# Attention ordered by query tile over all heads, v projection within its own batch, and batch 1 transposed on TensorE

## The chip, the cores and the metric

The kernel runs on one core of one Trainium2 chip. The metric is the device time of that core in microseconds (us); lower is better. Engines are named as in the profile: PE (TensorE, matrix products), PEld (its weight loads, which overlap PE: 12.83 us of them in a batch of 29.84 us in which PE is busy throughout), DVE (VectorE), ACT (ScalarE), POOL (GpSimd), SP (SyncE, which only issues DMAs here). The span of an execution is the time from its first instruction to its last; in these runs the time is the span plus 1.7 to 1.9 us (283.9 and 285.62, 262.4 and 264.19).

## The reference, cut to what matters

There are 8 batches, 16 query heads on 4 kv heads, 384 positions, head dimension 64, model width 1024. Attention comes first, then a gated feed-forward whose gate mixes the positions.

```python
k = np.repeat(k, group, axis=1); v = np.repeat(v, group, axis=1)      # group = 4
scores = np.matmul(q, k.transpose(0, 1, 3, 2)) / np.sqrt(D)
attn = softmax(scores)
x = (attn @ v).transpose(0, 2, 1, 3).reshape(B, S, H * D)
h = np.maximum(x @ w_in, 0.0);  u, v = h[..., :512], h[..., 512:]
v_n = (v - mean(v)) / np.sqrt(var(v) + 1e-06)
v_s = np.einsum('ts,bsd->btd', w_spatial, v_n) + b_spatial[None, :, None]
out = (u * v_s) @ w_out
```

## The kernel before

Each batch is a row of nine visits. A visit starts with two units of scores (two 64-row products each) and their exps on ScalarE, and then gets other PE work to fill the time of those exps. That work is: the value products and sums of exps (`values`, giving `sums` and `X`), the v half of the projection (`pv`), the spatial product with w_spatial (`psp`), the u half (`pu`) and the output product (`po`). Four PSUM buffers (`ps`) are shared by all of them, and VectorE or ScalarE frees them.

Before the change a value product covers one head over all 384 positions and a call of `values` four heads, so a batch has four calls with 384 columns:

```python
def values(b, gp, quad, part=None):
    ...
    def tiles(dst, weights):
        for t in range(NST):
            for i in range(4):
                half, j = i // 2, quad * 2 + i % 2
                nc.tensor.matmul(dst[32 * i : 32 * (i + 1), 0:S], weights(t, half),
                                 a[:, t, half, j * S : (j + 1) * S], ...)
    ...
VALUES_AT = {0: (-1, 1, 1), 3: (0, 0, 0), 5: (0, 0, 1), 8: (0, 1, 0)}

def feed_forward(b, vi):          # the feed-forward of batch b-1 and b-2 in the visits of b
    ...
    if vi == 1: do_v(b - 1, 0, 1)
    if vi == 2: do_v(b - 1, 2)
    ...
    if vi == 2: do_o(b - 2, 0)
    if vi == 3: do_o(b - 2, 1)
    if vi == 4: do_o(b - 2, 2, 3, 4)
    if vi == 5: do_o(b - 2, 5)
    if vi == 6: do_sp(b - 1)
    if vi == 7: do_u(b - 1, 0, 1)
    if vi == 8: do_u(b - 1, 2)
```

Batch 0 is ordered by hand on PE, POOL, SP and also DVE. From batch 1 on, DVE is left to the scheduler of the framework, which may place a DVE instruction anywhere that its dependences and its priorities allow:

```python
def load_w_in(c0, c1):            # 16 DMAs of 64 KB a half, on GpSimd's queue, casting to fp16
    for gp in range(2):
        for half in range(2):
            for quad in range(2):
                ...
                for jq in range(2):
                    nc.gpsimd.dma_start(...)

def cast_ws():                    # waits for the load of w_spatial
    for tt in range(NST):
        nc.vector.tensor_copy(ws16[:, tt, :, :], ...)

def first_visit(vi):              # batch 0
    ...
    if vi == 4:
        cast_k(1, nc.vector)
        cast_q(1, 0, nc.vector)
        load_ws()
        load_bias()
    if vi in (6, 7): transpose_k(1, vi - 6)
    if vi in (7, 8): transpose_q(1, 0, vi - 7)
    if vi == 8:
        values(0, 1, 0, 0)
        dma_transpose_q(1, 1)     # the second half of batch 1's q, by a DMA
        cast_ws()                 # the last DVE work ordered by hand

with tc.manual_schedule(engines={PE, POOL, SP, DVE}):
    ...                           # batch 0
with tc.manual_schedule(engines={PE, POOL, SP}):
    ...                           # batches 1 to 7
```

The softmax here doesn't subtract the row's maximum and nothing guards it: scores larger than these inputs give would overflow.

Of the kernel before, what the change touches and what calls it, by code (L numbers as in the profile page):

```python
# [19 lines left out]
def kernel(  # L20
# [19 lines left out]
    nc = tc.nc  # L40
# [50 lines left out]

    def load_k(b):
        k32 = ld.tile([P, HKV, NST * D], FP32, name=f"k32_{b}", tag="k32")
        nc.sync.dma_start(k32, k[b].rearrange("g (p t) d -> p g (t d)", t=NST))
        loaded["k32", b] = k32

    def load_v(b):
        v32 = ld.tile([P, HKV, NST * D], FP32, name=f"v32_{b}", tag="v32")
        nc.sync.dma_start(v32, v[b].rearrange("g (p t) d -> p g (t d)", t=NST))
        loaded["v32", b] = v32  # L100

    def load_q(b, gp, pieces=1):
        q32 = ld.tile([P, 2 * G, NST * D], FP32, name=f"q32_{b}_{gp}", tag=f"q32_{gp}")
        n = 2 * G // pieces
        for i in range(pieces):
            h0 = gp * 2 * G + i * n
            nc.sync.dma_start(
                q32[:, i * n : (i + 1) * n, :],
                q[b, h0 : h0 + n].rearrange("h (p t) d -> p h (t d)", t=NST),
            )  # L110
        loaded["q32", b, gp] = q32

    def cast_k(b, engine):
        k16 = qk16.tile([P, NGP, NST, 2, D], FP16, name=f"k16_{b}", tag="k16")
        k32 = loaded["k32", b].rearrange("p (gp h) (t d) -> p gp t h d", gp=NGP, t=NST)
        for gp in range(NGP):
            engine.tensor_copy(k16[:, gp], k32[:, gp])  # L117
        loaded["k16", b] = k16

    def cast_v(b, engine):  # L120
        v16 = qk16.tile([P, HKV, NST, D], FP16, name=f"v16_{b}", tag="v16", bufs=3)
        engine.tensor_copy(v16.rearrange("p g t d -> p g (t d)"), loaded["v32", b])
        loaded["v16", b] = v16

    def cast_q(b, gp, engine):
        q16 = qk16.tile([P, G, NST, 2, D], FP16, name=f"q16_{b}_{gp}", tag=f"q16_{gp}")
        q32 = loaded["q32", b, gp]
        for half in range(2):
            engine.tensor_copy(
                q16[:, :, :, half, :],  # L130
                q32[:, half * G : (half + 1) * G, :].rearrange("p j (t d) -> p j t d", t=NST),
            )
        loaded["q16", b, gp] = q16

    def load_first():


        k32 = ld.tile([P, HKV, NST * D], FP32, name="k32_0", tag="k32")
        q32 = ld.tile([P, 2 * G, NST * D], FP32, name="q32_0_0", tag="q32_0")

        def piece(queue, i):
            queue.dma_start(
                q32[:, 2 * i : 2 * i + 2, :],
                q[0, 2 * i : 2 * i + 2].rearrange("h (p t) d -> p h (t d)", t=NST),
            )

        def kpiece(gp):
            nc.sync.dma_start(
                k32[:, 2 * gp : 2 * gp + 2, :],
                k[0, 2 * gp : 2 * gp + 2].rearrange("g (p t) d -> p g (t d)", t=NST),  # L150
            )

        kpiece(0)
        piece(nc.scalar, 0)
        piece(nc.sync, 2)
        piece(nc.sync, 1)
        piece(nc.sync, 3)
        load_v(0)
        load_q(0, 1, pieces=2)
        kpiece(1)  # L160

        k16 = qk16.tile([P, NGP, NST, 2, D], FP16, name="k16_0", tag="k16")
        q16 = qk16.tile([P, G, NST, 2, D], FP16, name="q16_0_0", tag="q16_0")
        k32v = k32.rearrange("p (gp h) (t d) -> p gp t h d", gp=NGP, t=NST)
        q32v = q32.rearrange("p (h j) (t d) -> p j t h d", h=2, t=NST)
        nc.vector.tensor_copy(k16[:, 0], k32v[:, 0])  # L166
        nc.scalar.activation(q16[:, 0:2, :, 0, :], q32v[:, 0:2, :, 0, :], AF.Copy)
        nc.vector.tensor_copy(q16[:, 0:2, :, 1, :], q32v[:, 0:2, :, 1, :])
        nc.vector.tensor_copy(q16[:, 2:4, :, 0, :], q32v[:, 2:4, :, 0, :])
        nc.gpsimd.tensor_copy(q16[:, 2:4, :, 1, :], q32v[:, 2:4, :, 1, :])  # L170
        cast_v(0, nc.gpsimd)
        cast_q(0, 1, nc.gpsimd)
        nc.gpsimd.tensor_copy(k16[:, 1], k32v[:, 1])
        loaded["k16", 0] = k16
        loaded["q16", 0, 0] = q16

    def load_batch(b):
        load_k(b)
        load_q(b, 0)
        cast_k(b, nc.gpsimd)  # L180
        cast_q(b, 0, nc.gpsimd)
        load_v(b)
        load_q(b, 1)
        cast_v(b, nc.gpsimd)
        cast_q(b, 1, nc.gpsimd)

# [9 lines left out]
    def load_consts():  # L196
        make_identity(nc, ident16)
        nc.vector.memset(ones32, 1.0)
        nc.vector.memset(eps_t, eps_ln)

    def load_bias():
        nc.sync.dma_start(bias_b, moe_b_spatial.partition_broadcast(P))

    def load_w_in(c0, c1):

        for gp in range(2):
            for half in range(2):
                for quad in range(2):
                    r0 = (gp * 2 * G + half * G + 2 * quad) * D
                    rows = moe_w_in[r0 : r0 + 2 * D, c0:c1].rearrange(  # L210
                        "(jq jj r) n -> jq r jj n", jq=2, jj=2
                    )
                    kc = gp * 4 + quad * 2
                    for jq in range(2):
                        i = half * 2 + jq
                        nc.gpsimd.dma_start(  # L216
                            w_in16[32 * i : 32 * (i + 1), kc : kc + 2, c0:c1], rows[jq]
                        )
# [8 lines left out]
    def load_ws():  # L227
        ws32 = stage.tile([P, NST, S], FP32, name="ws32", tag="ws32", bufs=1)
        nc.sync.dma_start(ws32, moe_w_spatial.rearrange("(p tt) s -> p tt s", tt=NST))
        loaded["ws32"] = ws32  # L230

# [17 lines left out]
    kT, qT, aT, xT = {}, {}, {}, {}  # L249

    def dma_transpose_k(b):
        kT[b] = tr_sb.tile([P, NGP, NST, P], FP16, name=f"kT_{b}", tag="kT")
        nc.sync.dma_start_transpose(
            kT[b].rearrange("p g t q -> p (g t) q"),
            loaded["k16", b].rearrange("p g t h d -> p (g t h d)"),
        )

    def dma_transpose_q(b, gp):
        qT[b, gp] = tr_sb.tile([P, G, NST, P], FP16, name=f"qT_{b}_{gp}", tag=f"qT_{gp}", bufs=2)
        nc.sync.dma_start_transpose(  # L260
            qT[b, gp].rearrange("p j t q -> p (j t) q"),
            loaded["q16", b, gp].rearrange("p j t h d -> p (j t h d)"),
        )

    def transpose_k(b, gp):
        k16 = loaded[("k16", b)]
# [3 lines left out]
        if gp == 0:  # L270
            kT[b] = tr_sb.tile([P, NGP, NST, P], FP16, name=f"kT_{b}", tag="kT")
        nc.vector.tensor_copy(kT[b][:, gp], pk)

    def transpose_q(b, gp, jp):
        q16 = loaded[("q16", b, gp)]
        if jp == 0:
            qT[b, gp] = tr_sb.tile([P, G, NST, P], FP16, name=f"qT_{b}_{gp}", tag=f"qT_{gp}", bufs=2)
        pq = ps.tile([P, 2, NST, P], FP16, name=f"pq_{b}_{gp}_{jp}", tag="ps")
        for jj in range(2):
            for t in range(NST):  # L280
                nc.tensor.transpose(
                    pq[:, jj, t, :],
                    q16[:, 2 * jp + jj, t, :, :].rearrange("p h d -> p (h d)"),
                    ident16,
                )
        nc.vector.tensor_copy(qT[b, gp][:, 2 * jp : 2 * jp + 2, :, :], pq)

    def scores(b, units):
        scs = []
        for u in units:  # L290
            gp, c, t = u // 9, (u % 9) // 3, u % 3
            sc = ps_sc.tile([P, 2, 512], FP32, name=f"sc_{b}_{u}", tag="sc")
            rhs = qT[b, gp].rearrange("p j t q -> p (j t q)")
            for half in range(2):
                lo, hi = half * D, (half + 1) * D
                nc.tensor.matmul(  # L296
                    sc[:, half, :],
                    kT[b][lo:hi, gp, t, :],
                    rhs[lo:hi, c * 512 : (c + 1) * 512],
                    start=True,  # L300
                    stop=True,
                )
            scs.append((gp, c, t, sc))
        for gp, c, t, sc in scs:
            if (b, gp) not in aT:
                aT[b, gp] = att_a.tile(
                    [P, NST, 2, G * S], FP16, name=f"aT_{b}_{gp}", tag="aT"
                )
            nc.scalar.activation(  # L309
                aT[b, gp][:, t, :, c * 512 : (c + 1) * 512], sc, AF.Exp, scale=scale  # L310
            )

    def values(b, gp, quad, part=None):


        a = aT[b, gp]
# [147 lines left out]
    def do_v(b, *sts):  # L464
        for st in sts:
            mk_v(b, st)()
# [145 lines left out]
```

## Time and profile before

| Reading | Value | How to read it |
|---|---|---|
| Time | 267.97 us (266.47 to 268.8, three runs) | 268.38 with the run beside the changed kernel |
| Span of the profiled execution | 270.2 us, mean granted clock 0.983 | a longer execution than any fast run on record: those of this kernel have spans of 264.1 to 270.1 us and clocks of 0.986 to 1.0 |
| Steady batch | 29.84 us, all of it PE busy, clock 1.00 | PE bound; any PE time saved here counts six times. The mean of the six is 29.94; one of them takes 30.57, with a wait of 0.7 us for a DMA transpose |
| First scores of batch 1 | at 28.64 us | all of the start and batch 0 lie before it |

From the page of the kernel before: busy us of each engine, share of the span and instructions; then two rows of slices. The digits are tenths of busy time, one for each fortieth of the span (6.75 us); PEclk is the granted clock in the same way.

```profile
PE 250.0 (93%) x2233; PEld 109.6 (41%) x2233; DVE 139.0 (51%) x273; ACT 185.0 (68%) x250; POOL 54.4 (20%) x90
...
PE   1887993989999999999999899999999999999993
...
PEclk9998898899999999999999999999999999999998
```

PE is at 8 tenths or more from the eighth slice on, up to the last. What is left to win lies in the first seven slices, in the last one, or in doing less PE work.

One steady batch of the kernel before, from the table of stretches. The columns are the stretch, its length, then busy time and count of PE, PEld, DVE, ACT and POOL, the granted clock, the DMA share and GB/s.

```profile
59.82:89.66 29.84, 29.84 (x274) 12.83 (x276) 15.71 (x31) 23.29 (x32) 4.94 (x7) 1.00 0.63 174
```

PE has no idle time in it, and no other engine comes near 29.84 us.

The two waits of PE above 1 us, from the list of waits of the kernel before (total, times, longest, in us):

```profile
PE pk_0_158 L269 <- DVE k_0_129 L166: 4.5, 1, 4.5
PE sc_9_698 L296 <- DMA qT_1_464<-q_1_1_238: 4.1, 1, 4.1
```

The first is the start of the kernel. The second is batch 1 waiting for its second q half from the DMA transpose: the wait that the change sets out to remove.

VectorE around the end of batch 0 in the kernel before, from its timeline (start, busy us, then what it is; in brackets the idle time before it and what ended that):

```profile
18.94 1.02 DVE L129 CAST q_1_0_324<-q_1_0_192 128x768 f16<-128x768 f32 x2
...
29.74 1.90 DVE L236 CAST ws_466<-ws_327 128x384 f16<-128x384 f32 x3 [0.30 <-DMA ws_327<-in_moe_w_spatial_dram]
```

The casts for batch 1 are done by 20 us. The cast of w_spatial (`ws`) comes only when everything that batch 1 needs at its start is out of the way, and its data has landed by then; VectorE waited 0.3 us for it.

### The profile page before, as it was taken

Reading aid. Unit: us, or ns where it says so; the run is one execution under the profiler, and the core shown is the slowest. Engines: PE = TensorE matmul, PEld = TensorE weight load, DVE = VectorE, ACT = ScalarE, POOL = GpSimd, SP = SyncE. Lnnn points to the kernel's source line nnn. Section 1 sums busy time; section 2 is a strip of 40 time slices with the busy share of each in tenths; the row PEclk is TensorE's granted clock in tenths of the full one; section 3 lists DMA queues with packets and bytes.
Section 4 is the critical chain, followed back from the end, with each engine's and each line's share of the span. In section 5 each row is a group of like instructions: output and inputs, shape, how many; then the busy total and the mean of one; then the engine's idle time right before and its main releaser. Section 6 shows DMA issues by size and latency. Waiting matters only on the chain.

```text
span 270.2 us, 5397 instructions
## 1 busy us (share of the span) xinstructions
PE 250.0 (93%) x2233; PEld 109.6 (41%) x2233; DVE 139.0 (51%) x273; ACT 185.0 (68%) x250; POOL 54.4 (20%) x90
## 2 busy tenths in 40 slices
PE   1887993989999999999999899999999999999993
PEld 1333441434345434444344343443344433454541
DVE  3153644524466447634564447634564447744953
ACT  2799875597977777877977677877977777652000
POOL 1755823902500150004200150006100000000000
PEclk9998898899999999999999999999999999999998
DMA  6699999999137931599039932598039103200505
GB/s 209 172 261 296 291 79 200 165 177 317 31 157 182 282 111 69 185 182 296 2 155 188 278 114 93 173 213 253 2 155 206 22 0 155 80 1 2 233 0 233
DMA packets 57224, 42.03 MB, mean 156 GB/s; under 512 B 26736, under 2 KB 53488, under 8 KB 57200
## 3 DMA queue, kind: packets, MB, share of 16 engines
q1 hardware_dynamic: 53824, 38.34, 54.4%
q0 software_dynamic: 3104, 3.15, 7.6%
q8 instruction: 17, 0.28, 0.4%
q10 hardware_dynamic: 272, 0.20, 0.2%
q14 instruction: 7, 0.06, 0.1%
HBM read 25.95 MB, written 12.58 MB: 143 GB/s over the span
## 4 chain that ended last, share of the span: by engine, by line
PE 71%; DMA 19%; POOL 2%; SPq 2%; issue 1%; ACT 1%; DVE 1%; POOLq 0%
DMA w_in_105<-in_moe_w_in_dram 7%; DMA q_1_1_234<-in_q_dram 5%; DMA qT_0_798<-q_2_0_592 3%; DMA q_0_1_125<-in_q_dram 2%; DMA qT_0_2062<-q_5_0_1861 2%; ACT aT_1_1970 L309 1%; PE pv_0_3114 L359 1%; PE pv_0_2682 L359 1%; PE pv_0_2250 L359 1%; PE pv_0_1818 L359 1%; PE pv_0_1386 L359 1%; PE pv_2_1009 L359 1%; PE pv_0_954 L359 1%; PE pv_2_3150 L359 1%; PE pv_2_2737 L359 1%
## 5 line engine op out<-in xcount | busy, mean ns | idle before, releaser
L418 PEld LDWEIGHTS <-w_in_105 128*128 128x128 f16 x256 | 23.2, 98 | 21.5 <-issue 7.8
L216 POOL DMA_DIRECT2D w_in_105<-in_moe_w_in_dram x32 | 17.0, 539 | 11.7 <-DMA w_in_105<-in_moe_w_in_dram 11.7
L325 PEld LDWEIGHTS <-ones_102 128*32 128x32 f16 x384 | 7.5, 97 | 14.6 <-issue 12.8
L117 POOL CAST k_6_2290<-k_6_2286 128x384 f16<-128x384 f32 x2 | 1.0, 509 | 23.2 <-DMA k_6_2286<-in_k_dram 23.2
L117 POOL CAST k_5_1858<-k_5_1854 128x384 f16<-128x384 f32 x2 | 1.0, 509 | 21.9 <-issue 21.9
L117 POOL CAST k_7_2722<-k_7_2718 128x384 f16<-128x384 f32 x2 | 1.0, 509 | 21.6 <-DMA k_7_2718<-in_k_dram 21.6
L296 PEld LDWEIGHTS <-kT_162 64*128 64x128 f16 x36 | 2.1, 98 | 7.9 <-issue 6.7
L117 POOL CAST k_4_1426<-k_4_1422 128x384 f16<-128x384 f32 x2 | 1.0, 509 | 19.5 <-issue 19.5
L296 PEld LDWEIGHTS <-kT_394 64*128 64x128 f16 x36 | 1.3, 97 | 8.3 <-DMA qT_1_464<-q_1_1_238 4.4
L269 PE MATMUL pk_0_158<-ident_101,k_0_129 128*128 128x128 f16 x3 | 0.5, 306 | 4.5 <-DVE k_0_129 L166 4.5
L296 PE MATMUL sc_9_698<-qT_1_464,kT_394 64*128 64x512 f16 x2 | 0.4, 387 | 4.1 <-DMA qT_1_464<-q_1_1_238 4.1
L359 PEld LDWEIGHTS <-xt_267 128*128 128x128 f16 x24 | 2.3, 98 | 3.4 <-issue 1.0
L444 PEld LDWEIGHTS <-gT_3366 128*128 128x128 f16 x24 | 2.4, 98 | 2.8
L359 PEld LDWEIGHTS <-xt_1047 128*128 128x128 f16 x24 | 2.2, 98 | 3.2 <-issue 0.8
L359 PEld LDWEIGHTS <-xt_1911 128*128 128x128 f16 x24 | 2.2, 98 | 3.2 <-issue 0.8
L359 PEld LDWEIGHTS <-xt_2775 128*128 128x128 f16 x24 | 2.2, 98 | 3.2 <-issue 0.8
L359 PEld LDWEIGHTS <-xt_650 128*128 128x128 f16 x24 | 2.2, 98 | 3.2 <-issue 0.8
L359 PEld LDWEIGHTS <-xt_2343 128*128 128x128 f16 x24 | 2.2, 98 | 3.2 <-issue 0.8
L359 PEld LDWEIGHTS <-xt_1479 128*128 128x128 f16 x24 | 2.2, 97 | 3.2 <-issue 0.8
L444 PEld LDWEIGHTS <-gT_3618 128*128 128x128 f16 x24 | 2.3, 98 | 3.0 <-DVE gT_3618 L425 0.5
L444 PEld LDWEIGHTS <-gT_2093 128*128 128x128 f16 x24 | 2.1, 98 | 3.4 <-issue 1.3
L444 PEld LDWEIGHTS <-gT_1229 128*128 128x128 f16 x24 | 2.1, 98 | 3.3 <-issue 1.3
(1052 smaller groups left out, 742.8 us busy)
## 6 DMA issues: line engine op xcount, KB each, us to landing
w_in_105<-in_moe_w_in_dram POOLq DMA_DIRECT2D x32, 64.0 KB, 7.1
w_out_106<-in_moe_w_out_dram POOLq DMA_DIRECT2D x2, 512.0 KB, 7.4
q_0_1_125<-in_q_dram SPq DMA_DIRECT2D x2, 384.0 KB, 5.6
q_1_0_192<-in_q_dram SPq DMA_DIRECT2D x1, 768.0 KB, 7.0
q_1_1_234<-in_q_dram SPq DMA_DIRECT2D x1, 768.0 KB, 14.5
q_2_0_587<-in_q_dram SPq DMA_DIRECT2D x1, 768.0 KB, 14.4
q_2_1_597<-in_q_dram SPq DMA_DIRECT2D x1, 768.0 KB, 14.6
q_3_0_992<-in_q_dram SPq DMA_DIRECT2D x1, 768.0 KB, 7.1
```

The lines of the kernel that those rows point to most:

```text
L117: engine.tensor_copy(k16[:, gp], k32[:, gp])
L216: nc.gpsimd.dma_start(w_in16[32 * i : 32 * (i + 1), kc : kc + 2, c0:c1], rows[jq])
L269: nc.tensor.transpose(pk[:, t, :], k16[:, gp, t, :, :].rearrange("p h d -> p (h d)"), ident16)
L296: nc.tensor.matmul(sc[:, half, :], kT[b][lo:hi, gp, t, :], rhs[lo:hi, c * 512 : (c + 1) * 512], start=True, stop=True,)
L309: nc.scalar.activation(aT[b, gp][:, t, :, c * 512 : (c + 1) * 512], sc, AF.Exp, scale=scale)
L325: nc.tensor.matmul(dst[32 * i : 32 * (i + 1), 0:S], weights(t, half), a[:, t, half, j * S : (j + 1) * S], start=(t == 0), stop=(t == NST - 1),
L359: nc.tensor.matmul(pv, xt[:, kc, st * P : (st + 1) * P], w_in16[:, kc, DH:DFF], start=(kc == 0), stop=(kc == NKT - 1),)
L418: nc.tensor.matmul(pu[:, 0:S], w_in16[:, kc, mu * P : (mu + 1) * P], xT[b][:, kc, :], start=(kc == 0), stop=(kc == NKT - 1),)
L444: nc.tensor.matmul(po, gT[:, m, tt * P : (tt + 1) * P], w_out16[:, m, half * 512 : (half + 1) * 512], start=(m == 0), stop=(m == NDT - 1),)
```

## The change

The intent has five parts. (1) `values` works by query tile of 128 positions over all 16 heads, so that a column tile of the array is a kv head and each product has 512 columns: three calls a batch instead of four. (2) Two of the three v projections of a batch move into the batch itself, as soon as their query tile is done; only the third is left for the next batch. (3) All of batch 1's q is transposed by TensorE, so that no DMA transpose is waited for. (4) w_in is loaded by four large DMAs a half instead of sixteen small ones. (5) In passing, the casts of w_spatial move from the last visit of batch 0, where VectorE is ordered by hand, to visit 1 of batch 1, where it is not.

```diff
-    def values(b, gp, quad, part=None):
+    def values(b, qt):
         def tiles(dst, weights):
             for t in range(NST):
-                for i in range(4):
-                    half, j = i // 2, quad * 2 + i % 2
+                for g in range(HKV):
                     nc.tensor.matmul(
-                        dst[32 * i : 32 * (i + 1), 0:S],
-                        weights(t, half),
-                        a[:, t, half, j * S : (j + 1) * S],
+                        dst[32 * g : 32 * (g + 1), :],
+                        weights(t, g),
+                        a[:, g // 2, t, g % 2, :],
 ...
     def load_w_in(c0, c1):
-        for gp in range(2):
-            for half in range(2):
-                for quad in range(2):
-                    ...
-                    for jq in range(2):
-                        i = half * 2 + jq
-                        nc.gpsimd.dma_start(
-                            w_in16[32 * i : 32 * (i + 1), kc : kc + 2, c0:c1], rows[jq]
-                        )
+        for g in range(HKV):
+            nc.gpsimd.dma_start(
+                w_in16[32 * g : 32 * (g + 1), :, c0:c1],
+                moe_w_in[g * G * D : (g + 1) * G * D, c0:c1].rearrange("(kc r) n -> r kc n", r=32),
+            )
 ...
     def first_visit(vi):                       # batch 0
 ...
+        if vi == 5:
+            transpose_q(0, 1, 2)
+            for gp in range(NGP):
+                cast_k(1, gp, nc.vector)
+            load_w_in(0, DH)
+            for gp in range(NGP):
+                for half in range(2):
+                    cast_q(1, gp, 0, 1, half, nc.vector)
+        if vi == 6:
+            values(0, 1)
+            ...
+            load_w_out()
+        if vi == 7:
+            for gp in range(NGP):
+                transpose_k(1, gp)
+            do_v(0, 0, vector_relu=True)
         if vi == 8:
-            values(0, 1, 0, 0)
-            dma_transpose_q(1, 1)
-            cast_ws()
+            for gp in range(NGP):
+                transpose_q(1, gp, 0)
+            do_v(0, 1, vector_relu=True)
+    def visit(b, vi):                          # batch b and c = b - 1
+        if vi == 0: values(c, 2); do_o(c - 1, 1)
+        if vi == 1:
+            if b == 1:
+                cast_ws()
+                transpose_q(1, gp, 1)          # both gp
+            else:
+                do_o(c - 1, 2, 3)
+        if vi == 2: do_v(c, 2); do_o(c - 1, 4) # b == 1: transpose_q(1, gp, 2)
+        if vi == 3: values(b, 0); do_o(c - 1, 5)   # b == 1: transpose_ws(0, 1, 2)
+        if vi == 4: do_sp(c); do_u(c, 0)
+        if vi == 5: do_v(b, 0)
+        if vi == 6: values(b, 1); do_u(c, 1)
+        if vi == 7: do_u(c, 2, 3)
+        if vi == 8: do_v(b, 1); do_o(c, 0)
 ...
+        values(last, 2)
+        do_o(last - 1, 1, 2, 3)
+        do_v(last, 2)
+        do_o(last - 1, 4, 5)
+        do_sp(last)
```

(The diff is cut, and some `if` branches of `visit` are written on one line.) The diff does not show one consequence: in the instruction order of the built kernel, two of the three casts of w_spatial stand on VectorE ahead of the eviction of batch 0's last transposed q, and so ahead of batch 1's casts of k and q.

## The prediction

> **What bounds the kernel now.** TensorE. The page shows PE busy 250.0 of 270.2 us. The table of stretches gives a batch in the steady part 29.8 to 30.4 us, of which PE is busy all but 0 to 0.7 us at full clock. ScalarE is busy 23 us of that, VectorE 16. The 20 us in which PE idles are by its list of waits and timeline: 4.5 before the first transpose; about 6 in small waits while batch 0 runs at ScalarE's pace (one exp each 0.91 us); 4.1 at 41 us for the DMA transpose of batch 1's second q half; two waits of 0.7 for later DMA transposes; 4.7 after the last matmul. Half clock after the stalls at 26 to 28 and 46 to 48 us costs about 3 more.
>
> **Steady part, after.** The columns of the value matmuls are the same (4x9x384 = 3x9x512), 0.49 us a run of 12 becoming 0.64: three visits of about 2.0 us for four of 1.6, saving 0.1 to 0.2 us a batch with one change of array tiling. ScalarE's reciprocals fall from 8x0.5 to 6x0.6 us; off the path. Against that, the spatial product now comes two visits after the last v projection (before: four). The chain relu 0.6, statistics 0.9, rstd 0.5 behind two exps, three v_n, then two multiplies of 0.7 delays freeing of the four PSUM buffers; I estimate 0.5 us of new PE wait a batch. Net about +0.3 us a batch, +2 in all. At the end only two output chunks stand between the last v projection and the spatial product (before six, 5.2 us): the same chain of 4 us leaves about 2 us bare.
>
> **Start.** Transposing batch 1 on PE removes the 4.1 us stall and its slow clock, for 12 more transposes (0.7 us). Two v projections (3.5 us) move into batch 0. But VectorE's instruction order puts two casts of w_spatial ahead of the eviction of the last transposed q of batch 0 and of the casts of batch 1. They wait for the w_spatial load, which stands behind all of batch 0 and 1 in the sync queue. Before, that load landed at 29.7 us. Now w_in is issued from about 8 us in eight large pieces without waits in between, so it competes all along. [...] Of 5.3 MB about 2 land before w_in starts; 3.3 MB at 155 GB/s give a landing at about 30 us (27 to 34). PE runs dry at about 24, stays idle some 8 us, restarts at half clock, and batch 1's first scores come at about 43 us.
>
> **Sum.** 43 + 27.5 (batch 1 without output chunks) + 6x30.1 + tail 23 + 4.7 is 279 in the profile's span; unprofiled about 2 less, and I shade for the load landing earlier: **275.5 us, range 266 to 285**. Chances: faster 0.07, same 0.25, slower 0.68.
>
> **What would show it.** VectorE's cast of ws waits from about 18 to 30 us, and PE's wait for scores 15 of batch 0 ends with it; half clock after; no 4.1 us stall at batch 1; a steady batch of about 30.1 us with short waits of the spatial product for VectorE; a bare 2 us before the last spatial product.
>
> **What would make it wrong.** w_spatial landing by 24 us (the competing queue getting less than half): then the start gains and the time is 265 to 268. Or no wait at the spatial product: 2 to 4 us less.[...]

43 + 27.5 + 180.6 + 23 + 4.7 came to 278.8 us of span, and 2 and 1.3 off gave the 275.5. The 155 GB/s: the trace of the kernel before does not show it (204 GB/s, see the next section), so the 155 GB/s, and the half that the last paragraph speaks of, are the author's estimate. The half clock that the prediction counts on is in the trace of the kernel before: the granted clock was 0.50 from 26 to 28 us and from 46 to 48. So is its change of array tiling: there a run of twelve value products takes 0.49 us to the next start before another such run and 0.59 before a product of another tile size (131.26, 131.75, 132.34 us); that the tile size is the reason is not shown.

## The result, and the profile after

The changed kernel took 284.98 us (281.84 to 285.62, four runs) against 268.38 us. The ratio is 1.060, with a 95% interval of 1.052 to 1.067: it is slower by 6.0%. A ratio here is the mean time of one kernel's fast runs over that of the other's of the same rounds, so it is not quite the ratio of the medians quoted. The output is correct.

The stretches below run from mark to mark on PE: the first scores of batch 1, the first scores of batch 2, and the end of the last steady visit. Both columns are of the profiled executions; the forecast column is the sum in the prediction.

| Stretch (us) | Before | After | Forecast for after |
|---|---|---|---|
| Start to the first scores of batch 1 | 28.64 | 43.11 | 43 |
| Batch 1 | 31.18 | 31.82 | 27.5 |
| Six steady batches | 179.62 | 179.83 | 6 x 30.1 = 180.6 |
| End | 30.76 | 29.14 | 23 + 4.7 = 27.7 |
| Span | 270.2 | 283.9 | 278.8 |

The start holds all of the loss of 13.7 us between the two spans. The stretches do not hold quite the same work: after the change the start contains two v projections, 3.5 us at full clock, which the kernel before does in batch 1. Batch 1 has lost that work and the wait of 4.1 us, and is still 0.6 us longer.

The page of the changed kernel, the same lines as before (a slice is 7.1 us):

```profile
PE 255.3 (90%) x1957; PEld 103.9 (37%) x1957; DVE 140.3 (49%) x268; ACT 182.6 (64%) x232; POOL 43.1 (15%) x69
...
PE   2873188799999999999999999999999999999793
...
PEclk9998569979999999999999999999999999999799
```

In the fourth and fifth slices PE is now busy only 3 tenths and 1 tenth of the time, and the clock falls to 0.5 and 0.6 in the fifth and sixth. Two more stretches of lower clock, in the ninth slice and near the end, come up again below. PE has 276 fewer instructions, yet 5.3 us more busy time: part of it ran at half clock (granted 0.50 from 28 to 40 us, in which PE was busy for 4.65 us).

The waits of PE above 1 us in the changed kernel, without the start's 4.1:

```profile
PE sc L252 <- DVE qT L239: 10.7, 3, 9.7
...
PE psp L344 <- DVE v_n L328: 1.5, 1, 1.5
PE pv L306 <- DVE xt L290: 1.5, 1, 1.5
PE psw L196 <- DVE xt L290: 1.3, 1, 1.3
```

The DMA transpose has gone from the list, as intended. A wait of 9.7 us for a small copy on VectorE has come in its place. VectorE's timeline of the changed kernel says what that copy waited for:

```profile
18.16 0.42 DVE L239 COPY qT<-pq 128x512 f16<-128x512 f16 x1
32.25 1.24 DVE L187 CAST ws<-ws 128x384 f16<-128x384 f32 x2 [13.67 <-DMA ws<-in_moe_w_spatial_dram]
33.41 0.42 DVE L239 COPY qT<-pq 128x512 f16<-128x512 f16 x1
```

VectorE stands still for 13.67 us at a cast of w_spatial whose data lands at 32.2 us. The input of the 0.42 us copy behind it, `pq`, was done on PE at 20.33 us (19.93 and 0.40), yet the copy starts at 33.41, behind the two casts: VectorE took its instructions in order here, and everything for batch 1 waited too. PE, in its own timeline:

```profile
23.82 0.39 PE L252 MATMUL sc<-qT,kT 64*128 64x512 f16 x2
33.89 0.61 PE L252 MATMUL sc<-qT,kT 64*128 64x512 f16 x2 [9.68 <-DVE qT L239]
...
36.77 3.57 PE L306 MATMUL pv<-w_in,xt 128*128 128x512 f16 x8 [1.47 <-DVE xt L290]
...
41.29 1.89 PE L306 MATMUL pv<-w_in,xt 128*128 128x512 f16 x8
43.11 0.61 PE L252 MATMUL sc<-qT,kT 64*128 64x512 f16 x4
```

The first v projection takes 3.57 us and the second, the same work, 1.89: the price of the half clock after the idle stretch. The granted clock was 0.50 from 36.77 to 40.27 us, in the first, and 1.00 from 41.29 to 43.11, in the second. It had gone from 1.00 to 0.68 from 26 to 28 us and to 0.50 from 28 us, within the idle stretch. In the kernel before it was 0.50 from 46 to 48 us, after the wait of 4.1.

Why does the load land later than before (29.7 us)? The queue totals of the changed kernel from 16 to 26 us, while both queues were at work (packets as the profile counts them, MB, share of 16 engines' time); q0 is GpSimd's queue, which loads w_in and casts it, and q1 the sync queue, with the loads of batch 1 and then w_spatial:

```profile
q0 software_dynamic: 1330, 1.28, 76.2%
q1 hardware_dynamic: 1333, 1.01, 40.1%
```

The two queues moved the same number of packets, but not of bytes. The sync queue moved 1.01 MB in 10 us, 101 GB/s. The w_in queue wrote 1.28 MB of fp16, so it read twice that in fp32: an estimate of 256 GB/s (that its MB are of fp16 shows in the whole execution, where its 3.15 MB are the sizes of w_in and w_out in fp16). From 26 us to the landing at 32.2, with w_in all but done, the sync queue moved 1.47 MB, 237 GB/s. The prediction had counted on 155 GB/s for the sync queue, half of what it took both to move. From the trace of the kernel before: the queue moved 3.06 MB from 12 to 27 us, 204 of the 264 GB/s that all moved.

The steady batch ahead of PE, in the changed kernel:

```profile
116.66 1.04 PE L389 MATMUL po<-w_out,gT 128*128 128x512 f16 x4
117.63 0.60 PE L252 MATMUL sc<-qT,kT 64*128 64x512 f16 x4
118.17 2.53 PE L344 MATMUL psp<-wsT,v_n 128*128 128x384 f16 x12
120.63 1.46 PE L364 MATMUL pu<-xt,w_in 128*128 128x384 f16 x8
```

The spatial product's twelve matmuls take 2.46 us from start to the start of the next (118.17 to 120.63). In the kernel before the same twelve take 2.06 us to the next start (140.32 to 142.38). So a wait of 0.4 to 0.5 us hides inside the group. The list of waits does not show it; VectorE's timeline of the same stretch does:

```profile
116.75 1.46 DVE L328 TENSOR_SCALAR v_n<-v_r,mv,rstd 128x512 f16<-128x512 f32 x3 [1.44 <-ACT rstd L325]
118.12 1.28 DVE L290 TENSOR_TENSOR xt<-X,rec 128x512 f16<-128x512 f32 x2
119.32 0.68 DVE L396 COPY osb<-po 128x512 f32<-128x512 f32 x1
119.92 2.39 DVE L351 TENSOR_TENSOR v_s<-psp,bias_b 128x384 f32<-128x384 f32 x4
```

The three `v_n` come so late that the two multiplies which free the PSUM buffers of `X` start at 118.12, when the spatial product already wants four buffers.

### The profile page after: what moved, and what is told of

The parts are those of the page before. It is cut to its first block, busy times and chain, and to the rows that moved or that the text cites. A ratio compares the mean times of both kernels' runs of the same rounds, so it can differ in the third digit from the quotient of the medians.

```text
span 283.9 us, 4758 instructions
## 1 busy us (share of the span) xinstructions
PE 255.3 (90%) x1957; PEld 103.9 (37%) x1957; DVE 140.3 (49%) x268; ACT 182.6 (64%) x232; POOL 43.1 (15%) x69
## 3 DMA queue, kind: packets, MB, share of 16 engines
q0 software_dynamic: 2720, 3.15, 6.6%
## 4 chain that ended last, share of the span: by engine, by line
PE 81%; DMA 7%; SPq 3%; DVE 3%; ACT 3%; issue 1%; POOL 0%
PE pv L306 16%; PE pu L364 15%; PE po L389 15%; PE sc L252 12%; PE X L274 9%; PE psp L344 8%; PE sums L274 5%; DMA ws<-in_moe_w_spatial_dram 5%; SPq L122 2%; DMA q<-in_q_dram 2%; ACT aT L261 2%; DVE v_n L328 1%; DVE osb L396 0%; SPq L129 0%; DVE ws L187 0%
## 5 line engine op out<-in xcount | busy, mean ns | idle before, releaser
L261 ACT ACTIVATE aT<-sc 128x1024 f16<-128x1024 f32 x144 | 139.8, 1022 | 67.2 <-PE sc L252 67.2
L252 PE MATMUL sc<-qT,kT 64*128 64x512 f16 x288 | 46.6, 395 | 14.6 <-DVE qT L239 10.7
L306 PE MATMUL pv<-w_in,xt 128*128 128x512 f16 x192 | 47.2, 390 | 1.5 <-DVE xt L290 1.5
L290 DVE TENSOR_TENSOR xt<-X,rec 128x512 f16<-128x512 f32 x48 | 30.9, 685 | 33.4 <-ACT rec L286 30.7
L389 PE MATMUL po<-w_out,gT 128*128 128x512 f16 x192 | 47.4, 380 | 0.0
L364 PE MATMUL pu<-xt,w_in 128*128 128x384 f16 x256 | 45.8, 328 | 0.0
L274 PE MATMUL X<-aT,v 128*32 128x512 f16 x576 | 35.9, 385 | 0.0
L396 DVE COPY osb<-po 128x512 f32<-128x512 f32 x48 | 32.2, 682 | 1.5 <-PE po L389 1.5
L364 PEld LDWEIGHTS <-w_in 128*128 128x128 f16 x256 | 24.1, 99 | 22.0 <-issue 7.9
L159 POOL CAST q<-q 128x768 f16<-128x768 f32 (+2 forms) x32 | 23.4, 761 | 21.9 <-DMA q<-in_q_dram 14.9
## 6 DMA issues: line engine op xcount, KB each, us to landing
ws<-in_moe_w_spatial_dram SPq DMA_DIRECT2D x1, 576.0 KB, 14.1
```

What stands on the lines that cost most here:

```text
L159: engine.tensor_copy(dst, src)
L252: nc.tensor.matmul(sc[:, half, :], kT[b][lo:hi, gp, t, :], rhs[lo:hi, :], start=True, stop=True)
L261: nc.scalar.activation(aT[b, qt][:, gp, t], sc, AF.Exp, scale=scale)
L274: nc.tensor.matmul(dst[32 * g : 32 * (g + 1), :], weights(t, g), a[:, g // 2, t, g % 2, :], start=(t == 0), stop=(t == NST - 1),)
L290: nc.vector.tensor_tensor(xt[:, jj, :, qt * P : (qt + 1) * P], X.rearrange("p (j q) -> p j q", j=G), rec.rearrange("p (j q) -> p j q", j=G ...
L306: nc.tensor.matmul(pv, xt[:, kc, st * P : (st + 1) * P], w_in16[:, kc, DH:DFF], start=(kc == 0), stop=(kc == NKT - 1),)
```

## The experiments

Theory A was: VectorE's early casts of w_spatial hold up batch 0's last eviction, and the load that they wait for is late because w_in competes with it. The rival B was: the casts alone are at fault, and the start comes out clean once they are moved. A further possibility was that the new order of batch 1 and of the steady part costs the time.

### 1. The casts of w_spatial back at the end of batch 0

```diff
         if vi == 8:                # batch 0
             do_v(0, 1, vector_relu=True)
+            cast_ws()
 ...
             if b == 1:             # batch 1, visit 1
-                cast_ws()
```

> The changed kernel with one edit: the three casts of w_spatial are placed at the end of batch 0 in VectorE's hand-set order (as before had them), not left to the scheduler, which put two of them ahead of the last q eviction of batch 0. Theory A (two causes in series: VectorE waiting in order for the w_spatial load, and behind it loads of batch 1 that are themselves late because all of w_in now competes): PE's 9.7 us wait before scores 15 vanishes, but VectorE then waits for the second q half of batch 1 until about 28 us, so only 3 to 6 us are gained: 279 to 282 us. Rival B (the early cast alone is the loss): 10 us or more gained, 273 to 275 us. Rival C (the loss lies in the steady part, not in the start): no change, 284 to 285 us.

Measured: 277.62 us, ratio to before 1.030 (1.020 to 1.039); 7.4 us less than the changed kernel. That lies between A (279 to 282) and B (273 to 275) and meets neither. The wait of 9.7 us is gone. VectorE now waits for the other thing that the competition delays, batch 1's second q half, in this kernel's timeline:

```profile
29.00 0.50 DVE L159 CAST q<-q 128x256 f16<-128x256 f32 x2 [6.17 <-DMA q<-in_q_dram]
```

and PE in turn 4.6 us for `xt`, which VectorE makes after that cast. So the order is a cause, and not the only one.

### 2. Half of w_in issued one visit later

```diff
             for gp in range(NGP):
                 cast_k(1, gp, nc.vector)
-            load_w_in(0, DH)
 ...
+            load_w_in(0, DH)       # after the casts of batch 1, visit 6
             load_w_out()
```

> The changed kernel with one edit: the second half of w_in (needed only at about 55 us) is issued after the casts of batch 1, not before, so it no longer competes with the loads of batch 1 and of w_spatial. VectorE's early casts stay. Theory A: w_spatial lands at 26 to 28 us in place of 32.2, PE's wait before scores 15 falls from 9.7 to 4 to 6 us, time 279 to 281 us. Rival B (w_spatial is late because it stands last in the sync queue, whatever else is moved): it still lands at 31 to 32 us and the time stays at 284 to 285. Rival C: no change.

Measured: 279.18 us, ratio 1.033 (1.025 to 1.041): the time and the landing are as theory A expected. VectorE's order is that of the changed kernel; only the load is earlier:

```profile
26.82 1.22 DVE L187 CAST ws<-ws 128x384 f16<-128x384 f32 x2 [7.37 <-DMA ws<-in_moe_w_spatial_dram]
```

w_spatial lands at 26.8 instead of 32.2 us, VectorE's wait falls from 13.7 to 7.4, and PE's wait for the eviction from 9.7 to 3.4 (expected: 4 to 6). This shows that the late landing comes from the traffic of w_in. Whether that traffic weighs more because w_in is issued early or because its pieces are large is not shown: no run has the small pieces in the new kernel.

### 3. Both

The edits of 1 and 2 together.

> Both edits: w_spatial cast at the end of batch 0, second half of w_in issued after the casts of batch 1. Theory A: the gains add, PE waits for no load longer than 2 to 3 us in the start, 272 to 275 us. Rival B: the same as the first edit alone, 273 to 275, and the second edit adds less than 1 us. Rival C: 284 to 285 us. Under every theory that I hold the steady batch stays at 30.0 us, and the kernel stays slower than before (268.4) by 4 us or more, because of the bare wait at the end and the 0.5 us of new wait in each batch.

Measured: 272.02 us, ratio 1.006 (0.996 to 1.016), with one slow run of four among them; the median of the three fast runs is 270.88, below the 272 to 275 expected. The two gains add within the noise: 7.4 and 5.8 us alone, 13.0 together, or 14.1 with fast runs alone (of 16.6). The expectation that the kernel stays slower than before by 4 us or more failed: by the fast runs it is 2.0 us, and the interval of the ratio includes no difference. Most of the loss is thus in the start, and the new order of the rest can account for no more than what is left. Its profiled run was slow, so nothing is read from that profile. One expectation was taken from it, and experiment 5 is what came of it.

### 4. The kernel before, with the casts of w_spatial moved ahead

If the order of VectorE is the cause, it must hurt the kernel before as well, with none of the rest of the change.

```diff
         if vi == 4:
-            cast_k(1, nc.vector)
-            cast_q(1, 0, nc.vector)
             load_ws()
             load_bias()
+            cast_ws()
+            cast_k(1, nc.vector)
+            cast_q(1, 0, nc.vector)
 ...
             dma_transpose_q(1, 1)
-            cast_ws()
```

> The kernel before with one edit: the casts of w_spatial are put into VectorE's order ahead of the casts of batch 1, about where the changed kernel has them; nothing else of the change. Theories A and B: VectorE waits from about 18 us until w_spatial lands at about 29 us, PE runs dry and drops to half clock, and the time rises by 8 to 13 us to 276 to 281 us. Rival C (the place of these casts does not matter): 268 us as before.

Measured: 277.04 us with one slow run of four (280.48); the fast runs are 275.25, 275.27 and 278.81 us. The ratio of fast runs is 1.027 (1.014 to 1.040), a loss of 7.3 us, just under the 8 to 13 expected; the record classes it as unclear at its threshold of 2%, but it is above 1 clear of noise. The cast in its timeline of VectorE, and the longest wait in its list of PE's waits:

```profile
30.51 1.79 DVE L236 CAST ws<-ws 128x384 f16<-128x384 f32 x3 [11.62 <-DMA ws<-in_moe_w_spatial_dram]
```

```profile
PE pk L269 <- DVE k L117: 10.5, 1, 10.5
```

VectorE stands 11.62 us, PE 10.5, and the time rises by some 7 us. The same three instructions, in the wrong place of one engine's order, do this without any new attention code.

### 5. Experiment 3, with w_out loaded in batch 1

```diff
             load_w_in(0, DH)
-            load_w_out()
 ...
             if b == 1:             # visit 1
+                load_w_out()
```

> The two edits of the start together (w_spatial cast at the end of batch 0; second half of w_in after the casts of batch 1), and w_out issued after the loads of batch 2, because in the run with both edits PE still waited 2.8 us for w_in, which then shared the DMA engines with w_out, and restarted at half clock. Theory A: that wait goes, 267 to 269 us, level with before (268.9). If the wait for w_in is not due to w_out, it stays and the time is 272.

Measured: 271.62 us (269.66 to 273.82, the highest slow; median of the fast runs 270.7), ratio 1.013 (1.004 to 1.021). The gain expected (267 to 269 us) did not come; the interval overlaps that of experiment 3, so w_out is worth nothing that these runs can show. The wait of PE for w_in that it was to remove had been seen only in a profile of the slow state; in this run's profile, a fast one, it is absent. The kernel is kept as the base of the next three, which were run beside it on the same chip.

### 6. The end: two more output chunks between the last v projection and the spatial product

```diff
-        do_o(last - 1, 1, 2, 3)
+        do_o(last - 1, 1)
         do_v(last, 2)
-        do_o(last - 1, 4, 5)
+        do_o(last - 1, 2, 3, 4, 5)
         do_sp(last)
```

> As the run before in this set, with one edit at the end: the last v projection comes after one output chunk instead of three, so that four chunks instead of two stand between it and the last spatial product. My theory (the chain relu, statistics, rstd, v_n of about 4 us is bare there): PE's 1.5 us wait before the last spatial product goes, 1.5 to 3 us gained over that run. Rival (the end is set by the order of output chunks on VectorE and the final store, so work is only moved about): less than 0.5 us gained.

Measured: 269.37 us, 1.3 us less than the fast runs of experiment 5 by the medians and 2.3 by the ratios (1.004 against 1.013); the intervals overlap. In the changed kernel the end reads, in PE's timeline:

```profile
264.55 4.16 PE L344 MATMUL psp<-wsT,v_n 128*128 128x384 f16 x12 [1.52 <-DVE v_n L328]
```

in experiment 5, the base of this one:

```profile
250.27 2.71 PE L344 MATMUL psp<-wsT,v_n 128*128 128x384 f16 x12 [1.52 <-DVE v_n L328]
```

and in this one:

```profile
249.84 2.71 PE L344 MATMUL psp<-wsT,v_n 128*128 128x384 f16 x12
```

The wait of 1.52 us is covered by output chunks, and that is what the traces show this edit to remove. The half clock that made the product 4.16 us in the changed kernel's profile (granted clock 0.50 from 266 to 268 us) was already absent in that of experiment 5, with the same wait before it.

### 7. The steady part: the third v projection one visit earlier

```diff
             else:                  # visit 1
-                do_o(c - 1, 2, 3)
+                do_o(c - 1, 2)
+                do_v(c, 2)
         if vi == 2:
-            do_v(c, 2)
+            if c == 0:
+                do_v(c, 2)
             if c > 0:
-                do_o(c - 1, 4)
+                do_o(c - 1, 3, 4)
```

> As the first run of this set, with one edit in the repeated part: the third v projection of a batch comes one visit earlier (visit 1), output chunks 3 and 4 after it. My theory (the spatial product waits for PSUM buffers freed late, because v_n and the multiplies queue behind the statistics chain: 12 matmuls take 2.47 us instead of 1.96): the spatial product takes 2.0 us, the batch 29.4 to 29.6 us instead of 30.0, 2.5 to 3.5 us gained in all. Rival (VectorE's evictions of 0.6 us each bound the spatial product whatever comes before): batch stays 30.0.

Measured: 267.57 us, ratio 0.999 (0.992 to 1.005): 3.1 us less than the fast runs of experiment 5 by the medians, 3.8 by the ratios (expected: 2.5 to 3.5). The hidden wait of some 0.45 us in six batches makes 2.7 of it. Its steady batch is 29.52 us instead of 29.97, and PE's and VectorE's timelines of it show the hidden wait gone:

```profile
163.92 2.12 PE L344 MATMUL psp<-wsT,v_n 128*128 128x384 f16 x12
165.93 1.46 PE L364 MATMUL pu<-xt,w_in 128*128 128x384 f16 x8
```

```profile
160.53 1.45 DVE L328 TENSOR_SCALAR v_n<-v_r,mv,rstd 128x512 f16<-128x512 f32 x3
163.41 1.29 DVE L290 TENSOR_TENSOR xt<-X,rec 128x512 f16<-128x512 f32 x2 [1.42 <-ACT rec L286]
```

The spatial product takes 2.01 us to the next start. `v_n` is done some 1.4 us before the multiplies of `X`, which wait for ScalarE's `rec` alone and start 0.5 us before the spatial product instead of with it.

### 8. Experiments 6 and 7 together

> Both edits of the two runs before this. Theory: the gains add, 262.5 to 265 us, faster than the kernel before by about 2 per cent, since what the change set out to gain (fewer and longer value matmuls, filled start) then shows. Rival: 267 or more.

Measured: 266.55 us, ratio 0.994 (0.987 to 1.0005). The gains add, 4.2 us below the fast runs of experiment 5 by the medians and 5.1 by the ratios, but the 262.5 to 265 us expected was missed by 1.5 us; experiment 5 had begun higher than thought.

The next three ran on another chip than this one, beside runs of the kernel before of their own (median 267.52 there, 269.67 here), so their ratios compare better with this one's than their times do.

### 9. Experiment 8, with half of batch 1's q transposed by a DMA again

```diff
         if vi == 8:
-            for gp in range(NGP):
-                transpose_q(1, gp, 0)
+            transpose_q(1, 0, 0)
+            dma_transpose_q(1, 1)
 ...                                # visits 1 and 2 of batch 1: transpose_q(1, 0, qt) only
```

> On the version with the start, end and repeated part mended (266.5 us, span 264.8): one part of the change undone, the second q half of batch 1 is transposed by DMA again instead of by TensorE. My theory (in this order of work the half is needed four score tiles into batch 1, not nine, and the DMA transpose lands late beside w_in): a PE wait of 5 us or more for it at batch 1, 271 to 278 us. Rival (the transposes on TensorE cost as much as they save): 265 to 267 us, no wait over 1 us.

Measured: 270.82 us, ratio 1.012 (1.005 to 1.019): 4.3 us more than experiment 8 by the medians, 4.8 by the ratios. Both are just under what was expected, 271 us and a wait of 5. PE's waits have the wait of the kernel before back:

```profile
PE sc L252 <- DMA qT<-q: 3.9, 1, 3.9
```

So in the new order of work this part of the change is a gain of about 4 us, which the longer stall of the changed kernel hides.

### 10. Experiment 8, with batch 0's first two v projections in batch 1 again

```diff
-            do_v(0, 0, vector_relu=True)       # visit 7 of batch 0
-            do_v(0, 1, vector_relu=True)       # visit 8 of batch 0
 ...
+                do_v(0, 0)                     # visit 1 of batch 1
+                do_v(0, 1)
```

> On the same mended version: another part undone for the start, the first two v projections of batch 0 are run in batch 1 instead of within batch 0. My theory (two thirds of their 3.5 us fill time that PE has in any case while ScalarE sets the pace): 1 to 2.5 us lost, 267.5 to 269. Rival (they only move work from one place to another): 266 to 267.

Measured: 267.84 us, ratio 1.002 (0.996 to 1.008), 1.3 us more than experiment 8 by the medians, 2.2 by the ratios, and as expected. The intervals overlap, so the sign is likely and the size is not settled.

### 11. Experiment 8, with w_spatial's transposes spread over visits 1 and 2 of batch 1

```diff
                     transpose_q(1, gp, 1)
+                transpose_ws(0)
 ...
                     transpose_q(1, gp, 2)
+                transpose_ws(1)
+                transpose_ws(2)
 ...
-            else:                  # visit 3, behind values(1, 0)
-                for st in range(NST):
-                    transpose_ws(st)
```

> On the same mended version: the three transposes of w_spatial go into visits 1 and 2 of batch 1, ahead of the value matmuls, instead of behind them, where they waited 1.3 and 0.3 us for PSUM buffers that the multiplies of those values hold; in two of the profiles PE fell to half clock right after. My theory: both waits go and no half clock follows, 1.5 to 3 us gained: 263.5 to 265 us, ratio to before 0.975 to 0.985. Rival: the waits only move to the next tile, under 0.5 us gained.

Measured: 264.5 us (263.46 to 264.96), ratio 0.989 (0.985 to 0.994). It is the fastest of all. The time is in the range expected, the ratio is not (0.975 to 0.985): it is faster than the kernel before by 1.1%. Against experiment 8 the intervals of the ratios overlap, so the gain rests on the profiles: batch 1 takes 29.51 us instead of 31.68. The waits did not all go: 0.5 us at `psw` and 1.0 at the spatial product are left. All its five runs have a granted clock of 0.996 to 1.0.

### 12. The changed kernel itself, with the edit of 11 alone

```diff
+ the edit of experiment 11, on the changed kernel
```

> The changed kernel itself with one edit: the w_spatial transposes of batch 1 moved to visits 1 and 2, as in the last run. This measures the term that my prediction sized worst (batch 1 at 27.5 us; measured 31.8). My theory: the PSUM waits of 1.3 and 0.3 us and the half-clock stretch that follows (the spatial product of batch 1 takes 3.9 us where later ones take 2.5) make up about 3 of the missing 4.3 us: batch 1 takes 28.5 to 29.5 us and the time falls by 2 to 3.5 us to 281.5 to 283. Rival (batch 1 is long because ScalarE and loads hold it): batch 1 stays above 31 us, time unchanged at 284 to 285.

Measured: 282.26 us, ratio 1.046 (1.035 to 1.058), 2.7 us less than the changed kernel and as the theory expected; it ran on a chip of its own and the intervals overlap. Batch 1 is what it was to test. In the changed kernel, PE's timeline of batch 1 has at the last of them:

```profile
55.99 0.33 PE L196 MATMUL psw<-ident,ws 128*128 128x128 f16 x3 [1.28 <-DVE xt L290]
56.25 0.61 PE L252 MATMUL sc<-qT,kT 64*128 64x512 f16 x4
56.85 3.88 PE L344 MATMUL psp<-wsT,v_n 128*128 128x384 f16 x12
```

The three groups of transposes of w_spatial (`psw`) stand right behind `values`, when the PSUM buffers are taken, and wait for them twice, 0.33 us (not shown) and 1.28 us; the spatial product then runs at half clock (granted 0.86 from 56 to 58 us and 0.50 from 58 to 60). With the edit the granted clock is 1.00 from 50 to 62 us, and the same place reads:

```profile
43.77 0.61 PE L252 MATMUL sc<-qT,kT 64*128 64x512 f16 x4
...
56.73 1.84 PE L344 MATMUL psp<-wsT,v_n 128*128 128x384 f16 x10 [0.31 <-DVE v_n L328]
...
72.74 0.60 PE L252 MATMUL sc<-qT,kT 64*128 64x512 f16 x4
```

Its batch 1 lasts 28.97 us (43.77 to 72.74) instead of 31.82, within the 28.5 to 29.5 expected. Part of that is the half clock, which the same waits do not always bring. In experiment 5 the same place reads

```profile
43.41 0.33 PE L196 MATMUL psw<-ident,ws 128*128 128x128 f16 x3 [1.28 <-DVE xt L290]
...
44.27 2.31 PE L344 MATMUL psp<-wsT,v_n 128*128 128x384 f16 x12
```

with a granted clock of 1.00 from 38 to 48 us, and batch 1 lasts 30.12 us there. So of the 2.85 us an estimate of 1.7 is the half clock (31.82 less 30.12).

## Why the prediction was right or wrong

The direction and the mechanism were right; the size was too small: 275.5 us against 285, at the very end of its range of 266 to 285. The step that failed is the sum: its term for batch 1 (27.5 us, measured 31.82) and its step from the profile's span to the time (2 us taken off, where the time is the span plus 1.7). Term by term:

- **The cause in the start: right, and shown.** The prediction named the two casts ahead of the eviction and the late load. PE ran dry at 24 us and idled 9.7 us (forecast: some 8), at half clock afterwards (granted 0.50 from 28 to 40 us), with the first scores of batch 1 at 43.11 us (forecast: 43). Experiments 1 to 4 confirm both halves, the order and the traffic, and number 4 does so for the order without the rest of the change. That the 43 came out so exactly is luck: the load landed 2.2 us later than forecast, and from the landing to the first scores it took 10.9 us and not 13.
- **The load's landing: near, partly by luck.** "3.3 MB at 155 GB/s give a landing at about 30 us" assumed an even split; w_spatial landed at 32.2. From 16 to 26 us the split was even in packets, 1330 and 1333, and not in bytes: the sync queue had only 101 GB/s. So the even split of the bytes, the author's estimate, is not what the traces show. But w_in moved nothing before 11 us and little after 26, so over the whole stretch from 8 us to the landing the sync queue had an estimated 151 GB/s (the 5.3 MB less the 1.66 MB that had landed by 8 us, over 24.2 us). The rate was thus met in the mean, by a mixture that was not foreseen; short were the 2 MB said to have landed by then.
- **"27.5 (batch 1 without output chunks)": the term that was mis-sized most.** It took 31.82 us, 4.3 more. The prediction looked for waits in the steady part and at the end, but not at the three transposes of w_spatial, which the change put right behind `values` in batch 1 alone. Experiment 12 measures it: batch 1 is 2.85 us shorter without those waits of 1.6 us and the half clock after them. The remaining 1.5 us is mostly three waits in that run's batch 1 (0.54, 0.45 and 0.31 us).
- **The end, "leaves about 2 us bare": the wait was right, its aftermath was left out.** The wait was 1.52 us. The half clock after it (granted 0.50 from 266 to 268 us) was not in the sum: 29.14 us against 27.7. Experiment 6 took the wait away. The half clock is not a fixed price of it: of five profiles of fast runs with this wait (1.51 or 1.52 us), the product after it took 2.71 us in experiments 1, 2 and 5, and 4.16 and 3.55 in the changed kernel and experiment 12.
- **The steady part, "30.1 us": right.** 29.97 us, with a hidden wait of 0.45 us (2.46 less 2.01) at the spatial product (forecast: 0.5), 0.13 to 0.19 us over an undisturbed batch of the kernel before (29.78 to 29.84). Over all six batches the two kernels are level (179.83 and 179.62 us), mainly because one batch of the kernel before takes 30.57 us, with a wait of 0.7 us for a DMA transpose, and no batch of the changed kernel has such a wait. Experiment 7 removes the hidden wait and shows the gain that was intended: 29.52 us, some 0.3 us better than an undisturbed batch before. The saving in the value products is small, as forecast: a call took 1.58 us before (130.76 to 132.34) and takes 2.06 now (114.60 to 116.66), so four came to 6.3 us a batch and three come to 6.2. The change of array tiling in that forecast is seen as about 0.1 us: an output chunk that another follows takes 0.87 us to the next start (247.50 to 248.37 in the kernel before), and one that stands before scores 0.97 (116.66 to 117.63 here).
- **From the sum to the time: a wrong step.** The sum was 278.8 us of span. The prediction then took 2 us off, because the profiled span of the kernel before lay 2 us above its times. That span was of one of its longer executions (clock 0.983). For the run profiled after the change the time is the span plus 1.7. It also shaded down by 1.3 for an earlier landing, which did not come.

Those terms make up the gap to the profiled run's 285.62 us: batch 1 4.3, end 1.4, start 0.1, steady −0.8, offset 3.7, shading 1.3, together 10.0 of 10.1 us.

What the change itself was worth came out only after the start was mended. The DMA transpose removed: about 4 us (experiment 9). v within its own batch, in the start: perhaps 1.3 to 2.2 us (10). Steady batches: 0.3 us each once the wait is gone (7). All together the mended version (11) is 1.1% faster than the kernel before. Open are why experiment 5 gained nothing and what decides whether the half clock follows a short wait. Behind the waits of 0.33 and 1.28 us in batch 1 the spatial product took 3.88 and 3.87 us in the profiles of the changed kernel and experiment 8, and 2.3 us in those of experiments 1 and 5.

## What to carry to other kernels

An instruction that waited for a late load stopped everything behind it on VectorE here (for 13.67 us in the changed kernel, 11.62 in experiment 4), so when a cast leaves a hand-ordered block, read where the scheduler puts it in the built order: three casts of 0.66 us cost some 7 us here. Before adding up a forecast, look in every stretch for instructions that ask for a PSUM buffer right behind work that holds them all, and add the half clock that may follow even a short stall (here, behind a wait of 1.28 us, the product took 3.88 us in one profile and 2.31 in another). Before a forecast is moved from a profile's span to a time, check by clock and span whether the profiled execution was one of the longer ones.

## What these traces show of the clock, the queues and the span

- The half clock came with short waits too. In the changed kernel it was there at 57 to 60 us with no gap longer than 1.28 us (1.6 us of waits between 53.7 and 56.0), and at the end after a wait of 1.52 us. Three stretches of 2 us around the first in the trace of the changed kernel are below, in the columns named earlier (the clock is the third number from the end). The same waits in experiment 5's profile brought none (1.00 from 38 to 48 us, and a mean of 0.998 over the span), so in these runs it followed a short stall in some executions and not in others; why is not shown.

```profile
54.00:56.00 2.00, 0.39 (x5) 0.22 (x4) 2.00 (x5) 0.96 (x2) 0.00 (x0) 1.00 1.00 305
56.00:58.00 2.00, 2.00 (x12) 0.80 (x12) 1.44 (x5) 1.32 (x2) 0.96 (x2) 0.86 1.06 336
58.00:60.00 2.00, 2.00 (x8) 0.99 (x7) 1.42 (x3) 0.62 (x1) 1.15 (x2) 0.50 1.11 330
```

- Two queues with equal packets did not get equal bytes. From 16 to 26 us of the changed kernel they moved 1330 and 1333 packets; a casting load on GpSimd's queue read an estimated 256 GB/s (twice its 1.28 MB in 10 us) while the sync queue had 101, a ratio of about 2.5.
- An output chunk took 0.97 us to the next start before scores, which have another tile size, and 0.87 before another output chunk: about 0.1 us.
- The device time is the span from the first instruction to the last plus 1.7 to 1.9 us in these runs.
